# Attention row sums: the first add of a unit shared between VectorE and GpSimd, probability tiles laid out in halves

## The chip, the cores and the metric

The kernel runs on one core of a Trainium2 chip. The metric is device time in microseconds (us) of one execution. The engines are named as the profile names them: PE is TensorE (matmul), PEld its loading of weights, DVE is VectorE, ACT is ScalarE, POOL is GpSimd, SP is SyncE, which here only issues DMAs. An instruction "L1059" was recorded by line 1059 of the kernel before; in the changed kernel the lines of the attention loop have moved down by 2 to 15.

## The reference

```python
x = A_x                                   # 1 x 2048 x 1024, float32
x = x + _A_ref(_layernorm(x), A_wqkv, A_wo)               # attention, 32 heads of 32
x = x + _B_ref(_layernorm(x), B_w_r, B_w_gate, B_w_up, B_w_down)
x = x + _A_ref(_layernorm(x), A_wqkv, A_wo)               # the same weights again
x = x + _B_ref(_layernorm(x), B_w_r, B_w_gate, B_w_up, B_w_down)

# inside _A_ref
scores = einsum("bhqd,bhkd->bhqk", q, k) * Dh ** -0.5
p = softmax(scores, axis=-1)
o = einsum("bhqk,bhkd->bhqd", p, v)       # then @ wo
# inside _B_ref: a score per token, the 8 best tokens go through a SwiGLU FFN of
# width 3584, their result times sigmoid(score) is added to their rows
```

So there are two identical layers, each with a full softmax attention over 2048 tokens and 32 heads, and an FFN for eight tokens. Everything is float32. A softmax needs, for each head and query, the maximum over 2048 keys, the exponentials, and their sum; the change is about the sum.

## The kernel before, in words

Each layer (`layer(n, ...)`, n = 0 and 1) computes layer norm and the QKV product, stores q, k and v in DRAM, runs the attention, divides by the row sums, multiplies by wo (the out-projection), adds the residual and does layer norm and router scores. The FFN of a layer is spread over the work that follows.

**Units and steps.** The attention of a layer is cut into 8 groups of four heads and 4 chunks of 512 queries: 32 units. A unit goes through the 16 key tiles of 128 keys, so a layer has 512 steps, and both layers 64 units. In a step PE does, in this order: two products for the row maxima of a unit that comes 25 steps later (`pre_mm` for half of them, PSUM tiles named `st`), the eight score products of this step (`scores`, tiles `pre`), the other two products for the maxima, and the product P times v of the step before (`pv_step`). ACT writes exp(score - maximum) of the four heads to a tile `P[s]` of 128 keys x 2048 (4 heads x 512 queries); nine such tiles exist. DVE finds the row maxima in `st` (`dve.tensor_reduce`, four of 128x512 in a step); one of the four is first copied to SBUF by ACT (`first`). A product into an `st` tile has to wait until DVE has read the tile that used this bank before. In the last 24 steps of a layer no maxima are left to find, and three steps are done at a time.

**Row sums.** The sum over keys is a sum over 16 P tiles and then over 128 partitions. The table `SUMS` sets for each unit which P tiles are added by which means: "add" is a POOL add into a tile `acc` of 128x2048 (L1059), "merge" is a DMA on POOL's queue that adds one P tile onto another in memory (L1062), and tile 14 goes directly to the last product. An entry (16.5, "add", 9) is recorded at the end of the step 16 counted from the unit's start, with .5 as its rank among the entries of one step; step 16 is step 0 of the next unit. At step 22 (step 6 of the next unit, in the middle) `sum_mm` (L1069) multiplies tile 14 and `acc` by a block of ones: eight products of 512 columns, four heads side by side. Just after that, DVE combines the maxima of a unit (`nm_combine`, L732). Each engine carries out its instructions in the order in which they were recorded, so that an entry further down the table stands further back in POOL's row. Units 0 to 29 of a layer go by `SUMS`; unit 30 goes by `BEHIND_SUMS` and unit 31 by adds on DVE.

**Order around the change.** The loop over steps is written out by hand; `emit` records the entries of the table at the "mid" and "end" of a step. Loads queued by `queue_loads` and for wo (`load_wo`) are issued by SP one in a step. At the start of a layer's attention, `v` of the first group is loaded from DRAM. After the attention, the out-projection goes through 16 token tiles t: products (L1289), residual add, `split_o` (which scales and splits the attention output of tile t+2), `ln_stats`, `xn` (L1320), router score (L1322) and the last add on POOL (L1327). In tile 0 the reciprocals of the second half of the sums (`recip(second, 1)`) are also taken.

Of the kernel before, what the change touches and what calls it, by code (L numbers as in the profile page):

```python
# [8 lines left out]
F32 = mybir.dt.float32  # L9
# [3 lines left out]
AF = mybir.ActivationFunctionType  # L13
OP = mybir.AluOpType
# [5 lines left out]
NT = S // 128  # L20
# [3 lines left out]
NU = NG * QC  # L24
NS = NU * NT
EPS = 1e-5
SCALE = DH ** -0.5
# [5 lines left out]
LEAD = 25  # L33
PB = 9


SUMS = (
    (3, "merge", 2, 1), (5, "merge", 4, 3), (6, "add", 0, 5), (7, "add", 6), (9, "merge", 7, 8), (9.5, "add", 2), (11, "merge", 9, 10),
    (11.5, "add", 4), (12, "add", 11), (14, "merge", 13, 12), (14.5, "add", 7), (16, "merge", 14, 15), (16.5, "add", 9), (19.5, "add", 13))
DIRECT = (14,)  # L40

BEHIND_SUMS = (
# [2 lines left out]
BEHIND_DIRECT = (15,)  # L45
# [10 lines left out]
def unit_events(left):  # L56

    if left == 0:
        return [(k + 1, "mid", 1, "add", (k, 0 if k == 1 else None, True)) for k in range(1, NT) if k not in LAST_DIRECT]
    ev = []  # L60
    for at, what, k, *other in (SUMS, BEHIND_SUMS)[left == 1]:
        args = (k, *other) if what == "merge" else (k, *(other or [None]), what == "vadd")
        ev.append((int(at), "end", at % 1, "merge" if what == "merge" else "add", args))
    return ev + [(SUM_AT, "mid", 5, "sum", ())]


# [4 lines left out]
def tile_kernel(ctx, tc, x, wqkv, wo, w_r, w_gate, w_up, w_down, out):  # L71
# [581 lines left out]
    def layer(n, src, dst, prev=None, following=None):  # L653
# [365 lines left out]
        with sbuf(f"at{n}", bufs=2) as aw:  # L1019
# [23 lines left out]
            def pv_step(s):  # L1043
                u, kt = divmod(s, NT)
                g = u // QC
                if kt == 0:
                    PV[u] = ps_pv()
                for h in range(4):
                    pe.matmul(PV[u][32 * h:32 * h + 32, :], V[g][:, kt, 32 * h:32 * h + 32], P[s][:, h, :],  # L1049
                              start=(kt == 0), stop=(kt == NT - 1), tile_position=(0, 32 * h))  # L1050
                if kt == NT - 1 and u < NU - 1:
                    store_o(u, aw.tile([128, 512], F32, name="o"))

            def acc_add(u, k, first, on_dve):
                if u not in ACC:
                    ACC[u] = aw.tile([128, 2048], F32, name="acc")
                o = ACC[u]
                a = P[u * NT + first].rearrange("p h c -> p (h c)") if first is not None else o
                (dve if on_dve else pool).tensor_tensor(o, a, P[u * NT + k].rearrange("p h c -> p (h c)"), op=OP.add)  # L1059

            def merge(u, a, b):
                pool.dma_start(P[u * NT + a], P[u * NT + b], accum_op=OP.add)  # L1062

            def sum_mm(u):
                p = ps_st()
                parts = [P[u * NT + k] for k in (LAST_DIRECT, BEHIND_DIRECT, DIRECT)[min(NU - 1 - u, 2)]] + [ACC.pop(u).rearrange("p (h c) -> p h c", h=4)]
                for i, a in enumerate(parts):
                    for h in range(4):
                        pe.matmul(p[32 * h:32 * h + 32, :], ones32, a[:, h, :], start=(i == 0),  # L1069
                                  stop=(i == len(parts) - 1), tile_position=(0, 32 * h))  # L1070
                return p

            def store_o(u, o):
# [19 lines left out]
            def recip(t, i):  # L1093
                dve.reciprocal(t, t)
                dma(half_of(rd, i), t)

            fns = {"add": acc_add, "merge": merge, "sum": sum_out}

            def emit(s, where):
                u, kt = divmod(s, NT)  # L1100
# [12 lines left out]
            wop = None  # L1113
            def half_step(s, i, third=False):
                if i == 0:
                    P[s] = aw.tile([128, 4, 512], F32, name="P", bufs=PB)
                p = scores(*divmod(s, NT), i, third)
                act.activation(P[s][:, 2 * i:2 * i + 2, :].rearrange("p h c -> p (h c)"), p, AF.Exp, scale=SCALE)  # L1118

            shared = {}  # L1120

            def rest_of_step(s):
# [14 lines left out]
                    recip(shared["first"], 0)  # L1137
                if s < NS and kt == 0:
                    queue_loads(u)
                    if u == NU - 2:  # L1140
                        loads.extend((load_wo, a) for a in range(KD))
                if s == (NU - QC) * NT + 1:
                    right.close()
# [10 lines left out]
            for s in [*range(threes), *range(threes, NS, 3), *range(NS, NS + 14)]:  # L1154
# [18 lines left out]
                if pr:  # L1173
                    pre_mm(*pr, 1, False)
                t = s - 1 if s < NS - LEAD else s - 2
                if s != NS - LEAD and 0 <= t < NS:
# [15 lines left out]
        if True:  # L1192
# [81 lines left out]
            for t in range(NT - 2 if n else NT):  # L1274
# [17 lines left out]
                    next(nxt)  # L1292
                x2 = X.pop(t)
                dve.tensor_tensor(x2, p, x2, op=OP.add)
                low = split_o(t + 2) if t + 2 < NT else None
                if t == 0:
                    recip(second, 1)
                if t + 4 < NT:
                    load_o(t + 4)
                if nxt and t == NT - 1:  # L1300
                    next(nxt)
                mv, rs = ln_stats(x2)
                if low:
                    low()
                if first_stage and t == CT + 3:
# [147 lines left out]
```

## Time and profile before

| | us |
|---|---|
| median of 3 timed runs | 4411.48 (4407.85 to 4411.88) |
| the profiled execution: its time | 4412.62 |
| its span in the trace | 4410.9 |

| engine | busy us | share of the span |
|---|---|---|
| PE | 4365.2 | 99% |
| PEld | 2622.8 | 59% |
| DVE | 3178.0 | 72% |
| ACT | 2888.6 | 65% |
| POOL | 3212.1 | 73% |

"PEclk" of the page is the clock of PE that was granted, as a share of its higher level; over the whole execution it was 0.996. The page ends its chain of work 92% on PE. The shares are means over stages that differ: the attention takes some 1390 us of each layer, and there all four engines are over 90% busy. In the answers of the trace, "[1.55 <-PE st L709]" behind an instruction means that its engine sat idle for 1.55 us before it, until the `st` product of line 709 had ended; "x8" means eight instructions of one kind in a row, shown as one; a PE instruction counts twice where a float32 product is two passes.

### The profile page before, as it was taken

The page shows a single profiled execution, that of the slowest core. Times are in us where ns is not written, and L with a number is a line of the kernel's source. Part 1 is how long each engine was busy: PE and PEld are TensorE (multiplying, and loading weights), DVE is VectorE, ACT ScalarE, POOL GpSimd, SP SyncE. Part 2 cuts the span into 40 slices and gives each one's busy share as a digit, 9 for nine tenths or more (in the row PEclk, how much of TensorE's full clock was granted, in tenths as well). Part 3 has the DMA queues.
Part 4 walks back from the last instruction along what each step waited for, and adds up shares of the span by engine and source line. Part 5 has one row for each costly group of instructions (what it writes and reads, how often), then busy time and mean ns, then how long its engine had stood idle before and what let it go on. Part 6 is the DMA issues. An engine that isn't in the chain of part 4 may idle for free.

```text
span 4410.9 us, 74569 instructions
## 1 busy us (share of the span) xinstructions
PE 4365.2 (99%) x28753; PEld 2622.8 (59%) x28753; DVE 3178.0 (72%) x4983; ACT 2888.6 (65%) x3486; POOL 3212.1 (73%) x1293
## 2 busy tenths in 40 slices
PE   9999999999999999999999999999999999999998
PEld 7888755555555555548877787555555555555583
DVE  2211579999999999986522215899999999999863
ACT  3322279999999999970222222899999999999510
POOL 4444369999999999925633342899999999999152
PEclk9999999999999999999999999999999999999999
DMA  6757578988989989868698774889989889888598
GB/s 205 206 179 205 155 165 189 201 191 190 204 191 195 199 185 206 168 161 244 178 321 279 253 215 127 195 187 199 197 185 204 190 192 203 191 189 183 162 267 336
DMA packets 337794, 892.40 MB, mean 202 GB/s; under 512 B 44892, under 2 KB 161628, under 8 KB 281102
## 3 DMA queue, kind: packets, MB, share of 16 engines
q0 software_dynamic: 53312, 384.39, 43.6%
q1 hardware_dynamic: 275454, 476.43, 36.3%
q10 hardware_dynamic: 8672, 26.81, 2.3%
q8 instruction: 226, 3.70, 0.3%
q14 instruction: 130, 1.06, 0.1%
HBM read 384.34 MB, written 119.47 MB: 114 GB/s over the span
## 4 chain that ended last, share of the span: by engine, by line
PE 92%; DMA 3%; DVE 3%; issue 1%; POOL 1%; ACT 0%; SPq 0%; ACTq 0%; POOLq 0%; DVEq 0%
PE pv L1049 22%; PE pre L727 21%; PE st L845 18%; PE st L709 15%; PE pre L845 6%; PE pre L1289 5%; PE st L1069 2%; DVE acc L1059 1%; PE pv L552 1%; DMA ord<-rd 1%; PE pre L709 1%; DMA wor<-in_A_wo_dram 1%; PE pv L845 1%; PE pre L814 0%; DMA P<-P 0%
## 5 line engine op out<-in xcount | busy, mean ns | idle before, releaser
L719 DVE TENSOR_REDUCE nm<-st 128x1 f32<-128x512 f32 x3004 | 1965.4, 685 | 239.5 <-PE st L709 148.7
L1059 POOL TENSOR_TENSOR acc<-acc,P 128x2048 f32<-128x2048 f32 x420 | 2056.4, 4896 | 9.4
L1118 ACT ACTIVATE P<-pre 128x1024 f32<-128x1024 f32 x2016 | 1959.9, 1027 | 21.3 <-PE pre L727 10.7
L727 PE MATMUL pre<-q,ks 64*128 64x512 f32 (+1 forms) x8064 | 1119.6, 395 | 3.6 <-ACT P L1118 2.9
L1049 PE MATMUL pv<-P,v 128*32 128x512 f32 x8192 | 1091.5, 607 | 4.9 <-DMA v<-vd 4.9
L709 PEld LDWEIGHTS st<-ks,q 64*128 64x128 f32 x3916 | 497.3, 184 | 865.2 <-DVE nm L719 766.5
L709 PE MATMUL st<-ks,q 64*128 64x512 f32 x3916 | 898.9, 448 | 1.3 <-DVE nm L719 1.3
L727 PEld LDWEIGHTS pre<-q,ks 64*128 64x128 f32 (+1 forms) x8064 | 765.6, 186 | 166.5 <-ACT P L1118 29.2
L717 ACT COPY first<-st 128x512 f32<-128x512 f32 x912 | 536.0, 588 | 144.3 <-PE st L709 100.1
L719 DVE TENSOR_REDUCE nm<-first 128x1 f32<-128x512 f32 x912 | 617.9, 678 | 0.0
L1062 POOL DMA_DIRECT2D P<-P x366 | 374.7, 1024 | 172.7 <-PE st L709 152.1
L860 DVE TENSOR_TENSOR lo<-st,hi 128x512 fp32r<-128x512 f32 x128 | 88.4, 691 | 529.0 <-ACT hi L859 504.3
L780 POOL TENSOR_TENSOR ohl<-wraw,ord 128x2048 fp32r<-128x2048 f32 (+1 forms) x54 | 222.5, 4125 | 309.3 <-ACT ord L775 284.9
L780 POOL TENSOR_TENSOR wl<-wraw,wh 128x2048 fp32r<-128x2048 f32 (+1 forms) x54 | 222.5, 4124 | 303.5 <-ACT wh L779 295.0
L859 ACT CAST hi<-st 128x512 fp32r<-128x512 f32 x128 | 75.3, 589 | 489.6 <-PE st L845 486.4
L1049 PEld LDWEIGHTS pv<-P,v 128*32 128x32 f32 x8192 | 163.5, 108 | 272.2 <-issue 260.8
L1059 POOL TENSOR_TENSOR acc<-P 128x2048 f32<-128x2048 f32 x62 | 318.5, 5137 | 0.0
L171 POOL TENSOR_TENSOR rs<-mv,eps_c 128x1 f32<-128x1 f32 x64 | 28.5, 446 | 284.9 <-DVE mv L169 284.9
L1289 PE MATMUL pre<-woh,ohl 128*128 128x512 f32 x960 | 223.4, 390 | 3.8 <-DVE pre L1322 3.8
L1220 ACT CAST ohl<-ord 128x1024 fp32r<-128x1024 f32 x32 | 33.6, 1051 | 275.8 <-DVE ord L1211 124.1
L1289 PEld LDWEIGHTS pre<-woh,ohl 128*128 128x128 f32 x960 | 179.6, 188 | 44.3 <-issue 4.6
L845 PE MATMUL st<-xh,wh 128*128 128x512 f32 x512 | 201.2, 393 | 0.0
(393 smaller groups left out, 4424.9 us busy)
## 6 DMA issues: line engine op xcount, KB each, us to landing
P<-P POOLq DMA_DIRECT2D x366, 1024.0 KB, 9.6
wraw<-in_A_wqkv_dram SPq DMA_DIRECT2D x96, 1024.0 KB
q<-qh SPq DMA_DIRECT2D x256, 128.0 KB
ks<-kh SPq DMA_DIRECT2D x112, 256.0 KB
fw<-in_B_w_down_dram SPq DMA_DIRECT2D x17, 1024.0 KB
vd<-vn SPq DMA_DIRECT2D x32, 512.0 KB
qh<-hi SPq DMA_DIRECT2D x64, 256.0 KB
ql<-lo SPq DMA_DIRECT2D x64, 256.0 KB
```

The costliest lines, as they stand in the source:

```text
L709: pe.matmul(ps[b], Q[u][rows, i, 0, qt * 128:(qt + 1) * 128], KS[(u // QC) % 2][rows, i, 0, j * 512:(j + 1) * 512], start=True, stop=True, ...
L717: act.copy(side, ps[0])
L719: dve.tensor_reduce(NM[u][:, j, 2 * i + b:2 * i + b + 1, qt], side if b == 0 and side is not None else ps[b], axis=AX.X, op=OP.max, negate ...
L727: pe.matmul(p[:, b * 512:(b + 1) * 512], KS[(u // QC) % 2][rows, i, slot, kt * 128:(kt + 1) * 128], Q[u][rows, i, slot, :], start=(slot == ...
L780: pool.tensor_tensor(wl[:, sl], raw[:, sl], wh[:, sl].bitcast(F32), op=OP.subtract)
L845: pe.matmul(p, *pair(a, l, r), start=(a == 0 and k == 0), stop=(a == KD - 1 and k == 2))
L860: dve.tensor_tensor(lo, p, hi.bitcast(F32), op=OP.subtract)
L1049: pe.matmul(PV[u][32 * h:32 * h + 32, :], V[g][:, kt, 32 * h:32 * h + 32], P[s][:, h, :], start=(kt == 0), stop=(kt == NT - 1), tile_posit ...
L1059: (dve if on_dve else pool).tensor_tensor(o, a, P[u * NT + k].rearrange("p h c -> p (h c)"), op=OP.add)
L1062: pool.dma_start(P[u * NT + a], P[u * NT + b], accum_op=OP.add)
L1118: act.activation(P[s][:, 2 * i:2 * i + 2, :].rearrange("p h c -> p (h c)"), p, AF.Exp, scale=SCALE)
L1289: pe.matmul(p[:, bl], l[:, a, :], r[a][:, bl], start=(k == 0 and a == 0), stop=(k == 2 and a == KD - 1))
```

## The change

In units that go by `SUMS`, the first add (tiles 0 and 5) is made in two halves: DVE adds the half 1 (128x1024), POOL the half 0. At the end of the chain, POOL adds the half 1 of tile 14 into `acc` ("rest"). The sum product then needs tile 14 only in half 0: twelve products of 256 columns instead of eight of 512. For halves to be contiguous, P and `acc` are laid out as 128 x 2 halves x 4 heads x 256 queries; exp writes such pieces, and P times v reads a head's 512 queries as two pieces of 256. The add of tile 13 is recorded one step earlier (18.5 instead of 19.5).

Besides, the first P times v of a layer is recorded in step 2 instead of step 1; the 16 loads of wo are queued one unit later; and in tile 0 of the out-projection `recip(second, 1)` and `ln_stats` are recorded ahead of `split_o`.

```diff
-    ...  (16, "merge", 14, 15), (16.5, "add", 9), (19.5, "add", 13))
+    ...  (16, "merge", 14, 15), (16.5, "add", 9), (18.5, "add", 13),
+    (20.5, "rest", 14))
...
-                    pe.matmul(PV[u][32 * h:32 * h + 32, :], V[g][:, kt, 32 * h:32 * h + 32], P[s][:, h, :],
+                    pe.matmul(PV[u][32 * h:32 * h + 32, :], V[g][:, kt, 32 * h:32 * h + 32], P[s][:, :, h, :],
...
-                    ACC[u] = aw.tile([128, 2048], F32, name="acc")
+                    ACC[u] = aw.tile([128, 2, 4, 256], F32, name="acc")
+                o = flat(ACC[u], half)
+                a = flat(P[u * NT + first], half) if first is not None else o
+                (dve if on_dve else pool).tensor_tensor(o, a, flat(P[u * NT + k], half), op=OP.add)
+
+            def acc_halves(u, k, first):
+                acc_add(u, k, first, True, slice(1, 2))
+                acc_add(u, k, first, False, slice(0, 1))
+
+            def acc_rest(u, k):
+                acc_add(u, k, None, False, slice(1, 2))
...
+                spans = [(parts, slice(0, 1)), (parts[1:], slice(1, 2))] if left == 2 else [(parts, slice(0, 2))]
+                for parts, x in spans:
+                    for i, a in enumerate(parts):
+                        for h in range(4):
+                            pe.matmul(p[32 * h:32 * h + 32, 256 * x.start:256 * x.stop], ones32, a[:, x, h, :], start=(i == 0),
+                                      stop=(i == len(parts) - 1), tile_position=(0, 32 * h))
...
-                    P[s] = aw.tile([128, 4, 512], F32, name="P", bufs=PB)
+                    P[s] = aw.tile([128, 2, 4, 256], F32, name="P", bufs=PB)
                 p = scores(*divmod(s, NT), i, third)
-                act.activation(P[s][:, 2 * i:2 * i + 2, :].rearrange("p h c -> p (h c)"), p, AF.Exp, scale=SCALE)
+                act.activation(P[s][:, :, 2 * i:2 * i + 2, :].rearrange("p x h c -> p h x c"),
+                               p.rearrange("p (h x c) -> p h x c", h=2, x=2), AF.Exp, scale=SCALE)
...
-                    if u == NU - 2:
+                    if u == NU - 1:
                         loads.extend((load_wo, a) for a in range(KD))
...
+                if s == 2:
+                    pv_step(0)
+                if s not in (1, NS - LEAD) and 0 <= t < NS:
                     pv_step(t)
...
-                low = split_o(t + 2) if t + 2 < NT else None
                 if t == 0:
                     recip(second, 1)
+                    stats = ln_stats(x2)
+                low = split_o(t + 2) if t + 2 < NT else None
...
-                mv, rs = ln_stats(x2)
+                mv, rs = stats if t == 0 else ln_stats(x2)
```

What the table does to the rows of the engines is seen best where one unit's sum is made and the next unit's begins. DVE, around the combining of maxima in step 6 of a unit, before:

```order
L719 TENSOR_REDUCE nm<-st 128x1 x3
L719 TENSOR_REDUCE nm<-first 128x1
L719 TENSOR_REDUCE nm<-st 128x1 x2
L732 TENSOR_REDUCE nmc_124<-nm 128x16
L719 TENSOR_REDUCE nm<-st 128x1
L719 TENSOR_REDUCE nm<-first 128x1
L719 TENSOR_REDUCE nm<-st 128x1 x2
```

and in the changed kernel:

```order
L721 TENSOR_REDUCE nm<-first 128x1
L721 TENSOR_REDUCE nm<-st 128x1 x2
L734 TENSOR_REDUCE nmc_124<-nm 128x16
L1064 TENSOR_TENSOR acc<-P 128x1024
L721 TENSOR_REDUCE nm<-st 128x1
L721 TENSOR_REDUCE nm<-first 128x1
L721 TENSOR_REDUCE nm<-st 128x1 x2
```

DVE's half of the first add stands between the combining and the four maxima of step 7. POOL, from the add of a unit's tile 9 to the next unit's second add (the numbers tell tiles apart: P_4276 is tile 9, P_4408 tile 13, P_4571 and P_4637 are the next unit's 2 and 4, P_4669 and P_4503 its 5 and 0, P_4702 its 6), before:

```order
L1059 TENSOR_TENSOR acc_4191<-acc_4191,P_4276 128x2048
L1062 DMA P_4571<-P_4538 128x2048
L1059 TENSOR_TENSOR acc_4191<-acc_4191,P_4408 128x2048
L1062 DMA P_4637<-P_4603 128x2048
L1059 TENSOR_TENSOR acc_4741<-P_4669,P_4503 128x2048
L1059 TENSOR_TENSOR acc_4741<-acc_4741,P_4702 128x2048
L1062 DMA P_4753<-P_4794 128x2048
```

and in the changed kernel, where the numbers have moved by up to 7 (P_4440 is tile 14):

```order
L1064 TENSOR_TENSOR acc_4191<-acc_4191,P_4277 128x2048
L1064 TENSOR_TENSOR acc_4191<-acc_4191,P_4409 128x2048
L1074 DMA P_4572<-P_4539 128x2048
L1064 TENSOR_TENSOR acc_4191<-acc_4191,P_4440 128x1024
L1074 DMA P_4638<-P_4605 128x2048
L1064 TENSOR_TENSOR acc_4747<-P_4671,P_4504 128x1024
L1064 TENSOR_TENSOR acc_4747<-acc_4747,P_4704 128x2048
L1074 DMA P_4760<-P_4801 128x2048
```

The add of tile 13 has gone ahead of a merge, the half add of tile 14 stands between the two merges, and the first add of the next unit is half as wide. PE, around the sum, before:

```order
L709 MATMUL st<-ks_148,q_144 128x512 x2
L1049 MATMUL pv<-P,v 32x512 x4
L1069 MATMUL st<-P,ones_85 32x512 x4
L1069 MATMUL st<-acc,ones_85 32x512 x4
L709 MATMUL st<-ks_148,q_142 128x512 x2
```

and in the changed kernel:

```order
L711 MATMUL st<-ks_148,q_144 128x512 x2
L1051 MATMUL pv<-P,v 32x512 x4
L1084 MATMUL st<-P,ones_85 32x256 x4
L1084 MATMUL st<-acc,ones_85 32x256 x8
L711 MATMUL st<-ks_148,q_142 128x512 x2
```

The place of the sum is the same; eight wide products have become twelve narrow ones.

## Rows read from the trace of the kernel before

**Rows 1.** Busy time of each engine in two stretches, 1000 to 1100 us (the middle of the first layer's attention) and 575 to 580 us (its beginning). The columns are the stretch, its length, and busy us and instructions of PE, PEld, DVE, ACT and POOL; then the granted clock of PE, the busy share of the DMA engines, and GB/s.

```profile
1000.00:1100.00 100.00, 100.00 (x774) 50.73 (x774) 92.80 (x153) 91.78 (x114) 96.81 (x34) 1.00 0.88 187
575.00:580.00 5.00, 4.09 (x18) 2.04 (x20) 1.28 (x2) 1.12 (x2) 0.00 (x0) 0.51 0.78 238
```

**Rows 2.** The chain that ended last, in order of time, from 1064 to 1107 us: start, us, what.

```profile
1066.85 0.43 PE st L709 x2
...
1068.46 0.99 PE pv L1049 x8
1069.46 1.72 PE st L1069 x16
1071.17 0.43 PE st L709
...
1073.86 0.43 PE st L709 x2
...
1075.45 1.00 PE pv L1049 x8
...
1104.10 1.00 PE pv L1049 x8
```

**Rows 3.** The timeline of PE and DVE around a sum: start, us, engine, line, operation, out<-in; in brackets the idle time before it and who ended it.

```profile
1066.78 0.50 PE L709 MATMUL st<-ks,q 64*128 64x512 f32 x2
...
1069.86 0.26 DVE L732 TENSOR_REDUCE nmc<-nm 128x16 fp32r<-128x64 f32 x1
...
1071.67 0.69 DVE L719 TENSOR_REDUCE nm<-st 128x1 f32<-128x512 f32 x1 [1.55 <-PE st L709]
1072.35 0.69 DVE L719 TENSOR_REDUCE nm<-first 128x1 f32<-128x512 f32 x1
1072.95 1.28 DVE L719 TENSOR_REDUCE nm<-st 128x1 f32<-128x512 f32 x2
...
1073.79 0.18 PEld L709 LDWEIGHTS st<-ks,q 64*128 64x128 f32 x2 [0.84 <-DVE nm L719]
```

**Rows 4.** POOL's timeline over one unit, from the first add of one to the first add of the next (between the rows shown stand the adds and merges of rows left out).

```profile
1068.05 5.12 POOL L1059 TENSOR_TENSOR acc<-P 128x2048 f32<-128x2048 f32 x1
1073.25 4.59 POOL L1059 TENSOR_TENSOR acc<-acc,P 128x2048 f32<-128x2048 f32 x1
1077.78 0.87 POOL L1062 DMA_DIRECT2D P<-P  x1
...
1099.12 5.19 POOL L1059 TENSOR_TENSOR acc<-acc,P 128x2048 f32<-128x2048 f32 x1
1105.68 0.87 POOL L1062 DMA_DIRECT2D P<-P  x1 [1.37 <-PE st L709]
1106.29 4.90 POOL L1059 TENSOR_TENSOR acc<-acc,P 128x2048 f32<-128x2048 f32 x1
1110.87 1.17 POOL L1062 DMA_DIRECT2D P<-P  x1
1111.48 5.15 POOL L1059 TENSOR_TENSOR acc<-P 128x2048 f32<-128x2048 f32 x1
```

**Rows 5.** All first adds on POOL from 600 to 1850 us, as one group: count, shortest, median and longest in ns, start of the first and the last.

```profile
L1059 POOL TENSOR_TENSOR acc<-P x28: 5100/5126/5207, 633.4 to 1808.0; 128x2048 f32<-128x2048 f32 x28
```

**Rows 6.** Groups of instructions by line and shape over the whole execution: count | busy us, mean ns of one | idle time before them and what ended it.

```profile
L1118 ACT ACTIVATE P<-pre 128x1024 f32<-128x1024 f32 x2016 | 1959.9, 1027 | 21.3 <-PE pre L727 10.7 <-DMA P<-P 3.1 <-issue 1.0
...
L1059 DVE TENSOR_TENSOR acc<-acc,P 128x2048 f32<-128x2048 f32 x42 | 96.1, 2289 | 12.8 <-POOL acc L1059 5.7 <-ACT P L1118 2.5 <-DMA P<-P 0.9
...
L817 ACT CAST xh<-pre 128x1024 fp32r<-128x1024 f32 x20 | 20.4, 1019 | 14.2 <-PE pre L814 14.2
L1256 DVE TENSOR_TENSOR wol<-wor,woh 128x1024 fp32r<-128x1024 f32 x14 | 16.2, 1218 | 0.0
...
L1415 POOL TENSOR_TENSOR x<-x,xn 128x1024 f32<-128x1024 f32 x1 | 2.4, 2361 | 0.0
```

**Rows 7.** Places outside the attention where an operation of DVE and an add of POOL lie beside each other, and one where POOL's add lies alone (the first row), as rows of the timeline; the last row is the group of all multiplications of line 1211, with shortest, median and longest in ns.

```profile
2002.90 2.38 POOL L1327 TENSOR_TENSOR x<-x,xn 128x1024 f32<-128x1024 f32 x1
...
2104.10 2.39 POOL L1327 TENSOR_TENSOR x<-x,xn 128x1024 f32<-128x1024 f32 x1
2104.21 2.28 DVE L333 TENSOR_TENSOR v<-v,lt 8x1 f32<-8x1 f32 x1
...
4165.63 1.23 DVE L1322 SCALAR_TENSOR_TENSOR pre<-xn,wrb 128x1024 f32<-128x1024 f32 x1
4165.82 3.29 POOL L1327 TENSOR_TENSOR x<-x,xn 128x1024 f32<-128x1024 f32 x1 [1.01 <-DVE xn L1320]
...
4167.92 2.28 DVE L1211 TENSOR_TENSOR ord<-ord 128x1024 f32<-128x1024 f32 x1
...
L1211 DVE TENSOR_TENSOR ord<-ord x32: 1203/1217/2283, 1955.3 to 4295.5; 128x1024 f32<-128x1024 f32 x32
```

**Rows 8.** The timeline in step 6 of the first layer's first unit, which has no sum to make.

```profile
590.07 0.49 PE L709 MATMUL st<-ks,q 64*128 64x512 f32 x2
...
591.34 4.89 POOL L1059 TENSOR_TENSOR acc<-P 128x2048 f32<-128x2048 f32 x1
...
593.33 0.68 DVE L719 TENSOR_REDUCE nm<-st 128x1 f32<-128x512 f32 x1
```

**Rows 9.** PE's timeline at the first product P times v of each layer.

```profile
575.91 1.94 PE L1049 MATMUL pv<-P,v 128*32 128x512 f32 x8 [2.76 <-DMA v<-vd]
...
2756.74 1.93 PE L1049 MATMUL pv<-P,v 128*32 128x512 f32 x8 [2.16 <-DMA v<-vd]
```

**Rows 10.** The timeline near the end of the first layer's attention, and in tile 0 of its out-projection.

```profile
1902.53 1.94 ACT L1118 ACTIVATE P<-pre 128x1024 f32<-128x1024 f32 x2 [1.62 <-DMA P<-P]
...
1906.34 7.13 DVE L1059 TENSOR_TENSOR acc<-acc,P 128x2048 f32<-128x2048 f32 x3 [1.15 <-ACT P L1118]
...
1983.86 0.93 PE L1289 MATMUL pre<-woh,ohl 128*128 128x512 f32 x3 [0.81 <-DVE pre L1322]
```

**Rows 11.** Merges by their DMAs, from issue to landing, 600 to 1850 us, all of line 1062.

```profile
DMA to landing us min/median/max: 7.0/9.4/14.3
```

More of the change, by code (lines that the diff above doesn't have):

```diff
@@ L37 @@
 SUMS = (
-    (3, "merge", 2, 1), (5, "merge", 4, 3), (6, "add", 0, 5), (7, "add", 6), (9, "merge", 7, 8), (9.5, "add", 2), (11, "merge", 9, 10),
-    (11.5, "add", 4), (12, "add", 11), (14, "merge", 13, 12), (14.5, "add", 7), (16, "merge", 14, 15), (16.5, "add", 9), (19.5, "add", 13))
+    (3, "merge", 2, 1), (5, "merge", 4, 3), (6, "halves", 0, 5), (7, "add", 6), (9, "merge", 7, 8), (9.5, "add", 2), (11, "merge", 9, 10),
+    (11.5, "add", 4), (12, "add", 11), (14, "merge", 13, 12), (14.5, "add", 7), (16, "merge", 14, 15), (16.5, "add", 9), (18.5, "add", 13),
+    (20.5, "rest", 14))
 DIRECT = (14,)
@@ L60, in unit_events @@
     ev = []
-    for at, what, k, *other in (SUMS, BEHIND_SUMS)[left == 1]:
-        args = (k, *other) if what == "merge" else (k, *(other or [None]), what == "vadd")
-        ev.append((int(at), "end", at % 1, "merge" if what == "merge" else "add", args))
+    for at, what, *args in (SUMS, BEHIND_SUMS)[left == 1]:
+        if what in ("add", "vadd"):
+            args = (args[0], *(args[1:] or [None]), what == "vadd")
+        ev.append((int(at), "end", at % 1, "add" if what == "vadd" else what, args))
     return ev + [(SUM_AT, "mid", 5, "sum", ())]
@@ L1052, in pv_step, with flat, acc_add @@
                     store_o(u, aw.tile([128, 512], F32, name="o"))
-            def acc_add(u, k, first, on_dve):
+            def flat(t, half=slice(0, 2)):
+                return t[:, half].rearrange("p x h c -> p (x h c)")
+            def acc_add(u, k, first, on_dve, half=slice(0, 2)):
                 if u not in ACC:
-                    ACC[u] = aw.tile([128, 2048], F32, name="acc")
-                o = ACC[u]
-                a = P[u * NT + first].rearrange("p h c -> p (h c)") if first is not None else o
-                (dve if on_dve else pool).tensor_tensor(o, a, P[u * NT + k].rearrange("p h c -> p (h c)"), op=OP.add)
+                    ACC[u] = aw.tile([128, 2, 4, 256], F32, name="acc")
+                o = flat(ACC[u], half)
+                a = flat(P[u * NT + first], half) if first is not None else o
+                (dve if on_dve else pool).tensor_tensor(o, a, flat(P[u * NT + k], half), op=OP.add)
@@ L1061, in merge @@
+            def acc_halves(u, k, first):
[3 more added lines that the diff above has]
+                acc_add(u, k, None, False, slice(1, 2))
             def merge(u, a, b):
-                pool.dma_start(P[u * NT + a], P[u * NT + b], accum_op=OP.add)
+                pool.dma_start(flat(P[u * NT + a]), flat(P[u * NT + b]), accum_op=OP.add)
             def sum_mm(u):
                 p = ps_st()
-                parts = [P[u * NT + k] for k in (LAST_DIRECT, BEHIND_DIRECT, DIRECT)[min(NU - 1 - u, 2)]] + [ACC.pop(u).rearrange("p (h c) -> p h c", h=4)]
@@ L1067, in sum_mm @@
[L1067 to L1070, printed above, removed]
+                left = min(NU - 1 - u, 2)
+                parts = [P[u * NT + k] for k in (LAST_DIRECT, BEHIND_DIRECT, DIRECT)[left]] + [ACC.pop(u)]
+                spans = [(parts, slice(0, 1)), (parts[1:], slice(1, 2))] if left == 2 else [(parts, slice(0, 2))]
@@ L1095, in recip @@
                 dma(half_of(rd, i), t)
-            fns = {"add": acc_add, "merge": merge, "sum": sum_out}
+            fns = {"add": acc_add, "halves": acc_halves, "rest": acc_rest, "merge": merge, "sum": sum_out}
             def emit(s, where):
@@ L1175, in layer @@
                 t = s - 1 if s < NS - LEAD else s - 2
-                if s != NS - LEAD and 0 <= t < NS:
+                if s == 2:
+                    pv_step(0)
+                if s not in (1, NS - LEAD) and 0 <= t < NS:
                     pv_step(t)
```

## The prediction, made before the changed kernel had run

> **What bounds the kernel now.** I read the shares first, then the busy time by stretch, because the shares average over stages with different limits. In the middle of the attention PE is busy for all of 100 us at full granted clock, and DVE (93%), ACT (92%) and POOL (97%) nearly so [rows 1]. So I next read the chain of waits, which runs along PE alone there: maxima, scores, P times v [rows 2]. A unit lasts 43.50 us: 28 first adds start between 633.4 and 1808.0, which is (1808.0 - 633.4) / 27 [rows 5]. Last come the timelines of the step in which a sum is made; T below is the start of that step's first `st` product, 1066.78 [rows 3].
>
> PE works without a break, but on a short lead: its first `st` product of step 8 has its weights loaded at 1073.79, after DVE's maxima ended (idle 0.84 <-DVE) [rows 3]. DVE hands back a bank just in time. The only slack is the stop of DVE after the combining of maxima: it ends at 1069.86 + 0.26 = T + 3.34, and the next maxima start at T + 4.89 after 1.55 idle, because PE is busy with the sum [rows 3].
>
> **The change part by part.** *Sum product.* Sixteen instructions take 1.72 us [rows 2], that is four waves of four (four heads side by side, two passes each) of 0.43. A wave of half the columns is taken as 0.215; twelve products are six waves, 1.29 us. That removes 0.43 per unit, and as PE has no idle time in it, the 60 units save 25.8 us if nothing else gets late.
>
> *A rule weighed.* The row above shows 0.43 for a wave of 512 columns. The Trainium skill, "TensorE: Matmul & The Clock Gate", section "Back-to-back issue gap", says that the spacing of products is set by weight loads as well as by columns, 81 ns at 128 and 131 ns at 512. By it, interpolated (about 98 at 256) and scaled to the row's 0.107 per instruction, the sum would take an estimated 1.93 us in place of 1.29; no run here shows it.
>
> *POOL.* The half adds take 128x1024 at 2.36 alone [rows 6]. I take the wide adds, 5.12 for a first one and 4.59 for an undisturbed later one [rows 4], less the difference 4.59 - 2.36 = 2.23: 2.91 for the half first add and 2.36 for the rest. In sum POOL's work in a unit hardly changes (-2.23 + 2.36), but it moves. Before, POOL sits idle for 1.37 ahead of a merge at 1105.68 [rows 4]: this merge writes on the tile that P times v has just read, and follows its end (1104.10 + 1.00 [rows 2]) by 0.58. The like merge at 1077.78 has P times v of step 8 ahead of it (end 1075.45 + 1.00 [rows 2]), so it can start no earlier than 1076.45 + 0.58 = T + 10.25, or T + 9.82 once the sum is 0.43 shorter. From it to the next unit's first add are 1111.48 - 1077.78 = 33.70 less the idle 1.37, 32.33 [rows 4]; with the rest add and its gap (2.38) it is 34.71. With the unit's new 43.07 the first add then starts at T' + 9.82 + 34.71 - 43.07 = T' + 1.46, against T + 1.27 before (1068.05 [rows 4]). The removed idle time just pays for the rest add. The rest ends some 1.2 us before (the merge between them, 1.17 [rows 4], less overlap), well ahead of the sum at T + 2.68 [rows 2], so the sum doesn't wait.
>
> *DVE's half.* It takes 1.22, as another two-input operation of that shape does, or 1.145 as half of the wide add's 2289 ns [rows 6]; alone it would fit into the 1.55 idle. But it isn't alone: POOL's half runs from T + 1.46 to T + 4.37. Three places in this trace show what a two-input operation of DVE does beside a POOL add [rows 7]: the one of line 1211 took 2.28 instead of 1.217, ending 1.09 after POOL's add; the 8x1 one of line 333 took 2.28 and ended with POOL's; and the POOL add of 4165.82 took 3.29 instead of 2.38, ending 2.25 after DVE's of 4165.63 (whose end is 4166.86). So they exclude each other and the later one waits, until about 0.13 before POOL's recorded end (1.22 - 1.09). The Trainium skill, "SBUF — State Buffer", section "Who interferes with whom", calls this an exclusive lock between VectorE with two SBUF inputs and a reading GpSimd; the three rows agree.
>
> So DVE, ready at T + 3.34, is held to T + 4.37 - 0.13 = T + 4.24 and done at T + 5.46. Queued behind it on DVE are the four maxima of step 7. The first could start at T + 4.89 - 0.43 = T + 4.46 and now starts near T + 5.40; the third frees the bank that PE's step 8 waits for. It could start at 1072.95 (T + 6.17) - 0.43 = T + 5.74 [rows 3] and starts at about 5.40 + 0.60 + 0.60 = T + 6.60 (0.60 is the distance of two that wait for nothing, 1072.35 to 1072.95 [rows 3]). So PE's step 8 is 0.86 late. I take 0.8, with 0.5 (a POOL add that ends 0.3 earlier) and 1.15 (one that ends 0.3 later) as bounds, for the 58 units with a sum in that step: +46.4. POOL's second add waits for DVE's half too, and would reach its merge at 5.46 + 0.15 + 4.53 = T + 10.14 (4.53 from 1073.25 to 1077.78 [rows 4]), still before the pin of T + 9.82 + 0.8, so this costs nothing. For the first unit of a layer POOL starts at 591.34 = T + 1.27, without a sum, and the maxima follow at 593.33 = T + 3.26 [rows 8]; the add ends near T + 4.9, so these are late by about 1.6: twice 1.6 is +3.2.
>
> *P in halves.* Each exp writes pieces of 256 instead of a flat row. A cast of the same width into strided pieces takes 1019 ns against exp's 1027 [rows 6], so nothing. P times v reads two pieces of 256: no row shows it. A gain has no reason, since the columns are the same. Above, eight of its instructions take 1.00 where eight of the sum take 0.86 [rows 2]; were these 0.14 paid a second time for the second piece, it would be 0.14 x 976 steps = 137 us. I take 0, since the cast's row shows that strided pieces of an operand cost nothing there, and leave a small chance to the far end.
>
> *First P times v.* PE waits 2.76 and 2.16 us for v at the start of the layers [rows 9], and for some us after it the granted clock is at half (0.51, the lower of two levels [rows 1]), where P times v takes 1.94 for 1.0. One step later that wait is gone or shorter: -1.6 to -4.4 per layer, together -3.2 to -8.8, taken as -6. Next to be late are the scores of step 2, whose loads come before.
>
> *Loads of wo later; order in the out-projection.* Near the end ACT waits 1.62 for a merge and DVE 1.15 behind it [rows 10]; fewer transfers beside them may give 0 to -2.3, taken as -1. In tile 0 PE waits 0.81 for DVE [rows 10]; -0.8 in each layer, -1.6.
>
> *Merges and P tiles.* The merges at 1105.68 and 1110.87 [rows 4] would come 3.0 instead of 5.2 apart. They land 9.4 after issue at the median and 14.3 at most [rows 11]; the tile that is written next is free some 10.4 after issue, 1.5 less than before. Cover enough for the median, so 0; without cover it is rival D.
>
> **Sum.** -25.8 + 46.4 + 3.2 - 6 - 1 - 1.6 = +15.2. The profiled execution took 4412.62, so 4427.8; it lies 1.14 above the median, so the median becomes 4427. With 0.5 and 1.15 for the stall and both ends of the others, this case spans 4405 to 4452.
>
> **The rivals.**
> A, faster: POOL's half is over when DVE arrives. POOL would have to start before T + 0.57 (3.34 + 0.13 - 2.91). For it: the rest could be cheaper than thought, as the removed idle of 1.37 and the earlier add of tile 13 pull forward. Against it: the merge behind P times v at T + 9.82 pins POOL's start [rows 2, 4]. Then -25.8 + 2 (the first units) - 8.6 = -32: 4379. The same results if the two don't exclude each other inside the attention.
> B, no loss: POOL isn't held at that merge, and the two halves, one behind the other, become a loop with POOL's own row: 2.78 + 1.22 + 0.15 + 4.53 + 34.71 = 43.39 per unit, 0.11 less than now, to which PE settles. Then -0.11 x 58 - 0.9 + 3.2 - 8.6  (the two units in which only the sum gets shorter: -0.9) = about -12.7: 4399. For it POOL's 97% busy [rows 1]; against it the same pin.
> C, slower, the change doesn't do what it says: a product of 256 columns costs as much as one of 512 (0.107 per instruction, 24 instructions, 2.58). Then the sum adds 0.86 per unit, +52, while DVE's half lies under it: 52 + 3.2 - 8.6, about 4458. For it: weights are loaded for every product. Against: these loads are of 32 columns. It decides from a sum above about 2.1 us; the skill's 1.93 would leave the forecast nearly as it is, as the late maxima cover the difference.
> D, slower: merges closer together land later than the P tiles are wanted. From landings of some 12 us, ACT waits for a tile 0.7 to 1.4 in each unit, 45 to 90: about 4487. For it the DMA engines at 88% [rows 1]; against it the median of 9.4 [rows 11].
>
> **How the numbers follow.** The forecast has 0.57, A 0.17, B 0.12, C 0.05, D 0.05; the 0.04 left is for others, such as the pieces of P times v. What a measurement of this kernel tells from no change is about 0.2%, 8.8 us: below 4402.7 is faster, above 4420.3 slower. Faster: A 0.17, of B 0.07, 0.02 of the forecast's own low end and 0.01 else, 0.27. Same: of B 0.05, of the forecast 0.10, else 0.01, 0.16. Slower: 0.45 of the forecast, C and D 0.10, else 0.02, 0.57. The range from 4385 to 4455 leaves out most of A's low side, D and the far half of C.
>
> **What would show it.** The sum's row should read about 1.29 in place of 1.72. DVE's half add should show about 2.1 instead of 1.2, ending behind POOL's half add, which starts near T + 1.5; the first maxima of step 7 should start near T + 5.4, and PE's step 8 near T + 7.4. The unit's period should be 43.87. If the DVE add shows 1.2 and POOL's half begins before T + 0.6, A holds; a period of 43.4 with PE's idle spread means B; a sum of 2.5, C; ACT idle <-DMA P<-P in every unit, D. PE's waits for v should be gone from the starts of the attention. I would be wrong in the main if POOL's add were the one that is held, or if DVE's lateness were taken up by the banks of step 8.

## The result, and the profile after

The changed kernel takes 4437.59 us (median of 6 runs, 4433.62 to 4441.43) against 4410.48 before: 1.0061 times as long, with a 95% interval of 1.0049 to 1.0072. It is slower by 27 us; forecast were 15 us, in a range from 4385 to 4455. The profiled execution took 4435.65, which is 23.0 more than that of before.

First the shares, and the stretches of [rows 1] again (columns as there):

```profile
PE 4363.8 (98%) x29233; PEld 2642.3 (60%) x29233; DVE 3299.6 (74%) x5043; ACT 2895.6 (65%) x3486; POOL 3227.6 (73%) x1353
```

```profile
1000.00:1100.00 100.00, 99.33 (x784) 50.67 (x782) 95.78 (x154) 91.04 (x112) 96.35 (x34) 1.00 0.89 187
575.00:580.00 5.00, 4.87 (x43) 2.10 (x42) 3.79 (x7) 3.75 (x6) 0.00 (x0) 1.00 0.90 255
```

PE now has idle time in the middle of the attention, and DVE has gone from 92.8 to 95.8. At the beginning of the attention PE is at full clock, where it was at half.

The groups of the first add, 600 to 1850 us, answer to [rows 5] (count, then shortest, median, longest in ns):

```profile
L1064 POOL TENSOR_TENSOR acc<-P x28: 2662/2974/3006, 630.5 to 1817.9; 128x1024 f32<-128x1024 f32 x28
L1064 DVE TENSOR_TENSOR acc<-P x28: 2251/2302/3034, 632.3 to 1819.0; 128x1024 f32<-128x1024 f32 x28
```

DVE's half shows 2.30 us, nearly twice what an add of this width takes. The period of a unit, (1817.9 - 630.5) / 27, is 43.98 us against 43.50. The timeline of one unit shows why (T is 1068.91 here; start, us, engine, line):

```profile
1069.78 1.19 POOL L1074 DMA_DIRECT2D P<-P  x1
...
1070.40 2.99 POOL L1064 TENSOR_TENSOR acc<-P 128x1024 f32<-128x1024 f32 x1
...
1071.99 0.26 DVE L734 TENSOR_REDUCE nmc<-nm 128x16 fp32r<-128x64 f32 x1
1072.17 2.31 DVE L1064 TENSOR_TENSOR acc<-P 128x1024 f32<-128x1024 f32 x1
...
1074.40 0.68 DVE L721 TENSOR_REDUCE nm<-st 128x1 f32<-128x512 f32 x1
...
1074.65 4.57 POOL L1064 TENSOR_TENSOR acc<-acc,P 128x2048 f32<-128x2048 f32 x1 [1.26 <-DVE acc L1064]
...
1075.60 1.27 DVE L721 TENSOR_REDUCE nm<-st 128x1 f32<-128x512 f32 x2
...
1076.33 0.50 PE L711 MATMUL st<-ks,q 64*128 64x512 f32 x1 [0.32 <-DVE nm L721]
...
1079.58 0.88 POOL L1074 DMA_DIRECT2D P<-P  x1 [0.36 <-PE st L711]
```

POOL's half ends at 1073.39, DVE's at 1074.48, 1.09 later: DVE's record begins at once, but its work only when POOL's is nearly over. The maxima behind it start at T + 5.49, the third at T + 6.69, and PE's product that needs its bank comes late. POOL's later merge waits 0.36 at the pin behind P times v. The chain of waits leads astray at this place:

```profile
1071.59 1.34 PE st L1084 x24
...
1072.95 0.59 ACT sm L1094
1073.54 0.31 ACT first L719
...
1073.91 1.05 ACT P L1133
...
1075.01 1.28 DVE nm L721 x2
...
1076.33 0.50 PE st L711
```

It goes from the sum over ACT to the maxima. But the four maxima began with the one at 1074.40, right where the add ended, and the others followed it without a break. An experiment below (`c_reduce`) takes the add's wait away and leaves ACT's copy `first` where it is (T + 4.50 there, T + 4.52 here), and the maxima come earlier. The narrow sum takes 1.34 us in place of 1.72 [rows 2].

I added up the 23.0 us of the two profiled executions from the starts of the 64 sums, differences of after and before: beginnings of the attention -2.8 and -2.7; the 29 units behind the first in each layer +13.3 and +19.8; ends of the attention -4.3 and -2.8; out-projection of the first layer +6.4; all that follows in the second -4.5; QKV +0.6. The -4.5 was not traced to a part of the change.

### The profile page after: what moved, and what is told of

Read it like the earlier page. It is cut to its first block, busy times and chain, and to the rows that moved or that the text cites. A ratio compares the mean times of both kernels' runs of the same rounds, so it can differ in the third digit from the quotient of the medians.

```text
span 4433.8 us, 75774 instructions
## 1 busy us (share of the span) xinstructions
PE 4363.8 (98%) x29233; PEld 2642.3 (60%) x29233; DVE 3299.6 (74%) x5043; ACT 2895.6 (65%) x3486; POOL 3227.6 (73%) x1353
## 4 chain that ended last, share of the span: by engine, by line
PE 88%; DVE 6%; DMA 2%; ACT 2%; issue 2%; POOL 1%; SPq 0%; ACTq 0%; POOLq 0%; DVEq 0%
PE pv L1051 21%; PE pre L729 20%; PE st L847 17%; PE st L711 14%; PE pre L847 5%; PE pre L1307 5%; DVE nm L721 3%; PE st L1084 1%; DVE acc L1064 1%; ACT P L1133 1%; PE pv L554 1%; DMA ord<-rd 1%; PE pre L711 1%; DMA wraw<-in_A_wqkv_dram 1%; PE pv L847 1%
## 5 line engine op out<-in xcount | busy, mean ns | idle before, releaser
L1064 POOL TENSOR_TENSOR acc<-acc,P 128x2048 f32<-128x2048 f32 x480 | 2192.2, 4567 | 85.6 <-DVE acc L1064 73.2
L729 PE MATMUL pre<-q,ks 64*128 64x512 f32 (+1 forms) x8064 | 1140.5, 396 | 1.8 <-ACT P L1133 1.8
L711 PEld LDWEIGHTS st<-ks,q 64*128 64x128 f32 x3916 | 512.3, 184 | 883.5 <-DVE nm L721 813.7
L711 PE MATMUL st<-ks,q 64*128 64x512 f32 x3916 | 943.6, 447 | 27.8 <-DVE nm L721 27.3
L847 PE MATMUL st<-xh,wl 128*128 128x512 f32 x512 | 199.4, 389 | 0.0
```

Of the source, the lines that this page charges most:

```text
L711: pe.matmul(ps[b], Q[u][rows, i, 0, qt * 128:(qt + 1) * 128], KS[(u // QC) % 2][rows, i, 0, j * 512:(j + 1) * 512], start=True, stop=True, ...
L729: pe.matmul(p[:, b * 512:(b + 1) * 512], KS[(u // QC) % 2][rows, i, slot, kt * 128:(kt + 1) * 128], Q[u][rows, i, slot, :], start=(slot == ...
L847: pe.matmul(p, *pair(a, l, r), start=(a == 0 and k == 0), stop=(a == KD - 1 and k == 2))
L1064: (dve if on_dve else pool).tensor_tensor(o, a, flat(P[u * NT + k], half), op=OP.add)
```

## The experiments

Twelve kernels ran, each with five rounds beside the kernel before.

**The parts one by one.** `a_whole` undoes the sharing:

```diff
-    (3, "merge", 2, 1), (5, "merge", 4, 3), (6, "halves", 0, 5), (7, "add", 6), (9, "merge", 7, 8), (9.5, "add", 2), (11, "merge", 9, 10),
+    (3, "merge", 2, 1), (5, "merge", 4, 3), (6, "add", 0, 5), (7, "add", 6), (9, "merge", 7, 8), (9.5, "add", 2), (11, "merge", 9, 10),
...
-    (20.5, "rest", 14))
-  spans = [(parts, slice(0, 1)), (parts[1:], slice(1, 2))] if left == 2 else [(parts, slice(0, 2))]
+  spans = [(parts, slice(0, 2))]
```

> The changed kernel with the shared add, the rest add and the narrow sum undone (whole first add on POOL, tile 13 at 19.5 again, eight products of 512 columns); the layout of P in halves, the first P times v in step 2, the later loads of wo and the out-projection's order stay. Theory L (DVE's half is held by POOL's half, and that is the whole loss of the attention): the unit's period is back at 43.50 and the time is that of before less what the other parts gave in the trace (starts of the attention -4.4 each, ends -4.3 and -2.8, out-projections +6.4 and -4.5): about 4397. Rival S (the strided pieces cost PE or ACT): the period stays near 43.9, about 4425 to 4437.

The last entry of the table is (19.5, "add", 13) again. Measured: 4400.36 (ratio 0.9975, 0.9964 to 0.9985), and PE is busy throughout, with DVE and POOL as before:

```profile
1000.00:1100.00 100.00, 100.00 (x776) 50.92 (x772) 92.64 (x153) 91.63 (x114) 96.56 (x33) 1.00 0.88 187
```

In the second layer its sums stay level with those of before: over 27 units the distance changes by 0.11 us. So the layout in halves costs nothing, and the sharing costs 37 us (4437.59 less 4400.36), or 38.7 with each kernel taken against the kernel before that ran beside it (27.1 more and 11.6 less). The first layer's out-projection loses only 0.9 here, and what follows in the second layer gains nothing (+0.3): neither the +6.4 nor the -4.5 of the changed kernel shows without the sharing, although the expectation put both down to the other parts. The three other parts, each alone on the kernel before: `b_pv` (`pv_step(0)` in step 2), `b_wo` (`NU - 2` to `NU - 1`), `b_out` (the reciprocals and statistics ahead of `split_o`), diffs as in the section on the change.

> The kernel before with the first P times v recorded in step 2, nothing else. Theory: PE's wait for v at the start of both layers and the half clock behind it go, -4.4 each: about 4402. Rival: the wait only moves to the next step: 4410.

> The kernel before with the loads of wo queued one unit later, nothing else. Theory R (the order in the out-projection costs the 4.8 us of tile 0 in the first layer; the later loads only help the end of the attention): -7, about 4404. Rival W (the loads of wo, being later, make the loads of the out-projection late): +0 to +7, 4410 to 4418.

> The kernel before with the reciprocals and the statistics ahead of the split in tile 0 of the out-projection, nothing else. Theory R: the store of the reciprocals is issued late and the first layer's tile 0 waits some 4 us longer: about 4415. Rival W: the order gains its 0.8 per layer: 4409.

Measured against 4411.97: `b_pv` 4406.59 (0.9976 to 0.9994), `b_wo` 4405.44 (0.9976 to 0.9994), `b_out` 4413.62 (0.9999 to 1.0017, which decides nothing). The first gives 5.4, less than the 8.8 expected, and the second 6.5, as expected. In the trace of `b_wo` the gain lies at the ends of the attention (-3.9 and -2.4). The end of the first layer's attention, before:

```profile
1897.00:1903.00 6.00, 5.11 (x40) 1.95 (x32) 2.77 (x4) 3.00 (x4) 3.20 (x1) 1.00 1.03 252
1903.00:1911.00 8.00, 7.21 (x44) 2.65 (x40) 6.70 (x3) 5.74 (x7) 0.87 (x1) 0.79 0.91 270
```

and in `b_wo`, where the same work comes 0.3 us earlier:

```profile
1897.00:1903.00 6.00, 5.11 (x42) 2.01 (x32) 3.12 (x3) 4.91 (x6) 2.92 (x1) 1.00 0.67 136
1903.00:1911.00 8.00, 8.00 (x64) 3.64 (x66) 7.76 (x4) 7.20 (x9) 0.88 (x1) 1.00 0.47 100
```

The DMA engines fall from full to 0.67 and 0.47, PE does 64 instructions instead of 44 in the second stretch, and its granted clock stays full where it was 0.79.

**The lock by itself.** `c_reduce` lets DVE's half read one tile:

```diff
-  acc_add(u, k, first, True, slice(1, 2))
+  dve.tensor_reduce(flat(ACC[u], slice(1, 2)),
+      flat(P[u * NT + k], slice(1, 2)).rearrange("p (c o) -> p c o", o=1), axis=AX.X, op=OP.max)
```

> The changed kernel, in which DVE's half of the first add reads one tile alone: a maximum over an axis of length one, 128x1024 from tile 5 to acc, at the same place in DVE's row and with the same waits after it. Left out: the half 1 of tile 0 is missing from the row sums. Theory L (a DVE operation with two SBUF inputs and a POOL add exclude each other): it runs from T + 3.34 for about 1.2 us beside POOL's half, the next maxima start near T + 4.5, PE doesn't stop, the unit's period is 43.1, the time about 4380. Rival (the loss is DVE's extra work ahead of the maxima, whatever it reads): DVE's operation shows over 2 us, or the maxima are late all the same: period 43.9, 4437.

Measured: 4379.43 (0.9918 to 0.9946). The operation at the same place, with POOL's half still beside it:

```profile
L1068 DVE TENSOR_REDUCE acc<-P x29: 1200/1207/1214, 632.4 to 1838.3; 128x1024 f32<-128x1024 f32 x29
L1064 POOL TENSOR_TENSOR acc<-P x29: 2660/2963/3018, 630.5 to 1836.6; 128x1024 f32<-128x1024 f32 x29
```

POOL's row is the same as in the changed kernel, and DVE's takes 1.21 from T + 3.26; the maxima start at T + 4.46, the third at T + 5.74, PE's wait is gone, the median period is 43.07. These are the numbers that the prediction worked out for the case without a lock (T + 4.46, T + 5.74, 43.07). So in these units what cost the time was not an extra operation on DVE, but that it was an add of two SBUF tiles beside a POOL add. The run changes the number of inputs and the kind of operation together, and does not separate these two; `d_wait` below shows that an add of two tiles takes 1.22 at this place when POOL's half isn't beside it. The first unit of a layer is different, as DVE has no idle time there: from P times v of its tile 6 to that of its tile 7 PE takes 4.28 and 4.32 us in the changed kernel's two layers, 3.71 here and 2.60 in `a_whole`, so most of that loss is DVE's extra work.

**Other orders of the two halves.** `d_merge`: POOL's merge of tiles 4 and 3 goes behind its half. `d_wait`: DVE's half begins 8 columns earlier, so POOL's half waits for it. `d_five8`: as `d_merge`, with 5/8 on DVE. The table in `d_merge` and `d_five8`:

```diff
-    (3, "merge", 2, 1), (5, "merge", 4, 3), (6, "halves", 0, 5), (7, "add", 6), (9, "merge", 7, 8), (9.5, "add", 2), (11, "merge", 9, 10),
+    (3, "merge", 2, 1), (6, "halves", 0, 5), (6.5, "merge", 4, 3), (7, "add", 6), (9, "merge", 7, 8), (9.5, "add", 2), (11, "merge", 9, 10),
```

and the columns in `d_wait` (in `d_five8` they are 768:2048 and 0:768; `cols` adds a range of columns):

```diff
-                acc_add(u, k, first, True, slice(1, 2))
-                acc_add(u, k, first, False, slice(0, 1))
+                cols(u, k, first, True, slice(1016, 2048))
+                cols(u, k, first, False, slice(0, 1024))
```

> The changed kernel with the merge of tiles 4 and 3 behind POOL's half of the first add instead of ahead of it. POOL's half then starts 0.6 earlier, near T + 0.9. Theory L: the lock goes 0.6 earlier, DVE's half ends near T + 4.95, PE's stop shrinks from 0.84 to some 0.2, the period to 43.3, the time to about 4400. Rival (the lateness comes from the pin at the merge behind P times v, or the merge that is later holds a P tile): period 43.9 and 4437, or ACT idle <-DMA P<-P.

> The changed kernel with DVE's half 8 columns wider, into POOL's half, so that POOL's half has to wait for DVE's (the order is DVE, then POOL). Theory L: DVE's half shows 1.2 from T + 3.3, PE's stop behind the maxima goes; POOL's half starts near T + 4.5, 3 us later than before, the rest add reaches the sum late, and the sum waits some 0.3: period 43.4, time about 4407. Rival (POOL's own chain bounds the unit): period over 44, above 4440.

> The changed kernel with the merge of tiles 4 and 3 behind the shared add, and 5/8 of the add (1280 columns) on DVE, 3/8 (768) on POOL. Theory L: POOL's part runs from T + 0.9 to T + 3.3 and is over when DVE arrives at T + 3.3; DVE's part takes 1.45 and ends near T + 4.75, the maxima are late by 0.2, within PE's lead: period 43.1 to 43.2, time about 4385. Rival (DVE's extra work is the loss): DVE has 0.3 more to do than in the changed kernel, 4440.

Measured: 4380.41 (0.9922 to 0.9949), 4387.48 (0.9939 to 0.9966), 4383.07 (0.9925 to 0.9952); all are faster than before, and the first two by 20 more than expected. The groups of `d_merge`:

```profile
L1064 POOL TENSOR_TENSOR acc<-P x29: 2377/2655/2673, 629.1 to 1837.4; 128x1024 f32<-128x1024 f32 x29
L1064 DVE TENSOR_TENSOR acc<-P x29: 1347/1399/2049, 631.5 to 1839.7; 128x1024 f32<-128x1024 f32 x29
```

and of `d_wait`:

```profile
L1069 DVE TENSOR_TENSOR acc<-P x29: 1219/1222/1227, 631.8 to 1844.5; 128x1032 f32<-128x1032 f32 x29
L1069 POOL TENSOR_TENSOR acc<-P x29: 2370/2374/2387, 633.2 to 1845.9; 128x1024 f32<-128x1024 f32 x29
```

I had moved POOL's half with its 2.99 us. It is a shorter record elsewhere: 2.66 behind another add, 2.37 where POOL has waited (the last section says why). In `d_merge` it ends at T + 3.57 rather than T + 3.9 and holds DVE for only 0.2, in `d_wait` it ends at T + 7.01, early enough for the rest add to be ready for the sum. The median periods are 43.13, 43.15 and 43.09. In the first layer PE never waits for DVE's maxima, in the second twice in `d_merge` and in `d_five8`, up to 0.7 us. In `d_wait` it waits eight times in each layer for ACT, up to 0.5 us, and the mean period is 43.3, so POOL's later half isn't quite free.

**The out-projection of the first layer.** In four kernels (the changed one, `c_reduce`, `d_wait`, `d_five8`) the first load of x after the attention starts 2.9 us behind the start of the last sum, in the others so far from 2.3 ahead of it to 1.4 behind. In the program as built, the last P tile of the layer lies, in these four and in no other, in the buffer over whose memory this load goes. The traces agree: in these four SP waits 6 to 11 us for a product of the sum before this load, in the others it doesn't. `g_slot` is the changed kernel with the later merge in one unit of a layer, which moves the last P tile to another buffer; `after_again` is the changed kernel.

```diff
+OTHER = [(6, "end", 0.5, *e[3:]) if e[:2] == (5, "end") else e for e in EVENTS[2]]
...
-                    todo += [(kt + NT * back, pri, fn, args, v) for (k, pos, pri, fn, args) in EVENTS[min(NU - 1 - v, 2)]
+                    todo += [(kt + NT * back, pri, fn, args, v) for (k, pos, pri, fn, args) in (OTHER if v == NU - 3 else EVENTS[min(NU - 1 - v, 2)])
```

> The changed kernel, in which one unit of a layer (the one before the last two) has the merge of tiles 4 and 3 behind the shared add. That alone costs or gains under 1 us a layer, but it changes which of the nine P buffers the last P tile of the layer lies in: no longer the one on whose memory the first load of x is put after the attention. Theory X (the 6.4 us that the first layer's out-projection lost come from this load, which waits until the last P tile has been read by the last sum product): the load of x is issued some 3 us before where it was, counted from the last sum, and the out-projection is back to within 1 us of before's: about 5 less than the changed kernel. Rival R (the loss comes from the order of the reciprocals, or from the later loads of wo): no difference.

> The changed kernel once more, as it is, on the same chip, for the comparison with g_slot: 4437 as in its first runs; the start of x again some 2.9 us behind the start of the last sum.

Measured: 4428.48 (1.0033 to 1.0060) and 4437.79 (1.0055 to 1.0083). In `g_slot`:

```profile
1964.40 2.76 PE L1085 MATMUL st<-P,ones 128*32 128x512 f32 x24
1965.77 0.35 SPq L102 DMA_DIRECT2D x<-in_A_x_dram  x1
```

and in `after_again`:

```profile
1965.22 2.76 PE L1084 MATMUL st<-P,ones 128*32 128x512 f32 x24
...
1968.14 0.35 SPq L101 DMA_DIRECT2D x<-in_A_x_dram  x1
```

The load starts 1.4 behind the start of the sum in `g_slot`; in `after_again` it starts 2.9 behind it, when the sum's products of the P tiles are over (SP waits 11.9 for them). The other loads are queued behind it on SP. PE's longest wait in tile 0 for DVE (0.8 before [rows 10]) is 1.5 in `g_slot` and 5.3 in `after_again`, and the first layer's out-projection loses 1.4 us instead of 7.1, against that of before. The medians differ by 9.3, the two profiled executions by 5.7. So in the changed kernel this loss goes with where a buffer lay, and the order of the reciprocals, which `g_slot` keeps, is not its cause. The late load alone doesn't settle it, though: the four kernels with it lose 6 us (the changed one), 9 (`c_reduce`), 8 (`d_five8`) and only 2 (`d_wait`), counted from the last sum to the last product. What lies between the load and PE's long wait was not tried. In the changed kernel DVE waits there 4.1 us for the DMA that stores the reciprocals; in `d_wait` it doesn't wait for it.

**A better version.** `f_merge` is `d_merge` with the old order in the out-projection, `f_seven` has 9/16 of the add on DVE besides.

> The changed kernel with the merge of tiles 4 and 3 behind the shared add, and the order in tile 0 of the out-projection as before. Theory: the period stays at 43.12, the reorder was worth nothing or -1.6: 4378 to 4381. Rival (the reorder helps by its 0.8 a layer): 4382.

> The same with 9/16 of the shared add (1152 columns) on DVE and 7/16 (896) on POOL. Theory L: POOL's part ends 0.2 to 0.3 earlier, so that DVE isn't held: DVE's part shows 1.35 in place of 1.40 with 128 more columns, the maxima start by T + 4.6, the period is 43.08 to 43.12: 4377 to 4381. Rival (DVE's longer part is paid): 4384.

Measured: 4383.48 (0.9930 to 0.9957) and 4380.87 (0.9924 to 0.9951): neither can be told from `d_merge`. `f_seven` shows the lock gone, its DVE part 1.35 with 128 more columns; `d_five8` had shown that too, with 1.48 for 1280 columns. The period of `f_seven` is 43.13, not below that of `d_merge`, so the 0.2 for which DVE is still held in `d_merge` costs nothing that shows. The groups of `f_seven`:

```profile
L1069 POOL TENSOR_TENSOR acc<-P x29: 2223/2379/2403, 629.3 to 1837.3; 128x896 f32<-128x896 f32 x29
L1069 DVE TENSOR_TENSOR acc<-P x29: 1346/1348/1965, 631.8 to 1839.6; 128x1152 f32<-128x1152 f32 x29
```

With 26 to 29 us less than before and some 54 to 57 less than the changed kernel, the same idea pays once the two halves don't meet.

## Why the prediction was right, and where it was off

**The mechanism.** Right in each step: POOL's half starts at T + 1.50 (forecast 1.46) because the merge behind P times v pins it, DVE's half ends at T + 5.58 (5.46), the third maxima start at T + 6.70 (6.60), the period is 43.97 in the median (43.87). The +1.6 for the first unit of each layer came out as 1.7, against `a_whole`; its own figures (1.27 + 2.91 - 0.13 + 1.22) put the end of that add at T + 5.27 rather than the 4.9 that was written, and it was measured at T + 5.06. `c_reduce` shows that without the lock the period is 43.07, as worked out. "The later one waits, until about 0.13 before POOL's recorded end" held: 1.22 less 1.09. The Trainium skill, "SBUF — State Buffer", section "Who interferes with whom", says that a VectorE instruction with at most one SBUF input, outside the two-port modes, doesn't contend with GpSimd; `c_reduce` agrees with its 1.21 beside POOL's 2.96.

**The narrow sum.** 1.29 was forecast, 1.34 measured; the rule of the Trainium skill, "TensorE: Matmul & The Clock Gate", section "Back-to-back issue gap", would have given an estimated 1.93, which the trace doesn't show. Rival C falls, and so do A and B for this order of the halves; `d_five8` and `f_seven` are rival A brought about, and `d_merge` nearly (4380 to 4383, where A had 4379). D falls: the merges land after 8.1 us at the median, earlier than before [rows 11].

**The step that failed, first.** "For the 58 units with a sum in that step: +46.4", less 25.8: 20.6 was forecast for the attention, 33.1 measured. Of this, 58 x (43.97 - 43.51) is 26.7: the stop of PE costs 0.90 in a unit (43.97 - 43.07), where 0.86 had been worked out and was rounded to 0.8 for no reason; the narrower sum gives 0.44 (43.51 - 43.07) for the 0.43 forecast. The rest are a few units that lose more. Three lose 0.4 to 0.7 more than the others, and two in the second layer lose 3.4 and 3.3 where the others lose 0.46 (the same two in `g_slot` and `after_again`). In the unit before the first of these, POOL waits at a merge where it otherwise doesn't; its half then starts 1.4 late, DVE's half is done later, PE stops for longer, and after that its granted clock is lower:

```profile
3026.75 0.89 POOL L1074 DMA_DIRECT2D P<-P  x1 [1.33 <-PE st L711]
...
3046.28 3.75 DVE L1064 TENSOR_TENSOR acc<-P 128x1024 f32<-128x1024 f32 x1
...
3050.68 0.49 PE L711 MATMUL st<-ks,q 64*128 64x512 f32 x1 [1.02 <-DVE nm L721]
```

```profile
3053.00:3056.00 3.00, 3.00 (x15) 0.79 (x13) 1.89 (x4) 1.81 (x2) 1.74 (x1) 0.53 0.53 138
```

Just after waits of 1.02 and 0.70 the granted clock is 0.53, about the lower of its two levels (1.2 GHz). I had reckoned with 58 units that are all alike. What held that merge was not tried.

**Second.** "-0.8 in each layer, -1.6" in the out-projection: the first layer lost 6.4 instead, which goes with the place of the last P tile, and the second, with all that follows, gained 4.5. I had costed moved instructions and not that a changed table gives buffers out in another order. The 0.8 per layer of the reorder is within the noise of `b_out`. Why the second layer gained stays open.

**Third, the other way.** "0 to -2.3, taken as -1" for the loads of wo: 6.5 measured. I counted the two waits shown [rows 10] and not PE's own idle time and its lower clock there: without the loads PE is busy for 8.00 of the 8 us from 1903 to 1911 instead of 7.21, at a granted clock of 1.00 instead of 0.79. The first P times v was right: -6 forecast, -5.4 measured.

In sum, by the timed runs: +23.8 was forecast for the sharing, with the first units, and it costs 38.7 (the changed kernel lies 27.1 above the kernel before that ran beside it, `a_whole` 11.6 below; some 6 of it go with the buffer); -8.6 was forecast for the rest, and it gives 11.6 (4411.97 less 4400.36). So 27 came out where 15 were forecast. (Of the span given with the forecast, 4405 was counted from the median before and 4452 from the profiled execution, which is 1.14 higher; this changes nothing.) That the total is nearer than the sharing alone, and stayed inside the range, is in part luck: the unforeseen losses and the gains at the ends of the attention and in the second layer partly cancel.

## What to carry to other kernels

Before giving VectorE an add of two SBUF tiles beside GpSimd adds, look in the trace for the time at which GpSimd's own add is over: shared work that starts together runs one after the other, while an order in which one part is over, or waits, kept the gain or most of it (4380 and 4387 us, against 4379 without the lock). When a table of events changes, look where the last tiles come to lie and which first load of the next stage goes over them. Transfers taken out of a stage whose DMA engines are full can be worth more than the waits that the trace names there.

## What was not expected of the hardware

An add on POOL has a longer record behind a merge than elsewhere: the same 128x1024 add shows 2.97 behind one, 2.66 behind another add, and 2.37 after idle time. The record overlaps the one ahead of it: in the timeline of the changed kernel the merge lasts until 1069.78 + 1.19 = 1070.97 and the add's record begins at 1070.40. The overlap is 0.57 behind a merge and 0.32 behind an add at the median. Counted from the end of the record ahead, the add takes 2.41 and 2.33, about the 2.37 that it takes after idle time, so the add itself isn't slower. This is why a shift of 0.6 us in POOL's row took 0.9 off the time at which the lock went: an add's end is better reckoned from the end of the record ahead of it than from its own start.
